# Decoding weights in 1024-column pieces, a one-operation low part of q, and the softmax guard on GpSimd, in a fused attention and two-layer MoE kernel

## The chip, the core and the metric

The kernel runs on one core of a Trainium2 chip. The metric is the time of one execution on the device, in microseconds, as the median of several runs. The engines are TensorE (PE in the profile, with its weight loads as PEld), VectorE (DVE), ScalarE (ACT), GpSimd (POOL) and SyncE (SP, which only issues DMAs here). Each engine works through its own instructions in a fixed order and waits for the others at semaphores.

## The reference

Inputs are float32. Attention with a forget gate runs on 4 batches, 8 heads, 576 positions and a head size of 64; its output, as 2304 tokens of 512 features, goes through two dense two-matrix layers with 2048 hidden features.

```python
def _attn_ref(q, k, v, f):
    scores = scale * np.matmul(q, k.transpose(0, 1, 3, 2))
    log_f = np.log(np.clip(f, 0.0001, 1.0))
    cum = np.cumsum(log_f, axis=-1)
    decay = cum[:, :, :, None] - cum[:, :, None, :]
    scores = np.where(causal, -1000000000.0, scores + decay)
    scores = scores - np.max(scores, axis=-1, keepdims=True)
    attn = np.exp(scores)
    attn = attn / (np.sum(attn, axis=-1, keepdims=True) + 1e-09)
    return np.matmul(attn, v).astype(np.float32)

def _moe_ref(x, w_in, w_out):
    h = x @ w_in
    return np.maximum(0.01 * h, h) @ w_out

def _moe2_ref(x, w_in, w_out, alpha):
    h = x @ w_in
    return (np.maximum(h, 0.0) + alpha * np.minimum(h, 0.0)) @ w_out
```

## The kernel before, in words

**Products of split numbers.** Most matrix products are made from a high and a low part of each float32 operand: the high part is a rounded copy (a "cast"), the low part is the rest (a "sub"), and three products of parts are added up in PSUM. Every operand of such a product therefore costs a cast and a subtraction on ScalarE, VectorE or GpSimd first. The first 16 heads of attention ("native", `NAT = 16`) are computed in plain float32 instead and need no split.

**Weights.** The weights arrive as 64-bit numbers. `assemble` (L481) loads a piece of 512 columns for 128 rows (512 KB) into a buffer of the ring `raw` (four buffers), then makes float32 of it in a buffer of the ring `cv` (three): ScalarE or GpSimd rescales the high word (`rebase`, L492 or L494), and VectorE shifts (`bits`, L499), adds the sign (`sign`, L502) and the low bits (`low`, L507). `split_w` (L518) then casts and subtracts into the buffer that TensorE reads. `weight1` (L530) does so for the 32 pieces of the first layer (16 chunks `f` of the hidden features, two halves each: the half of `w_in` and the half of `w_out`), all of them wanted by the first block of tokens; 18 of them are also written to DRAM and read back for later blocks. `weight2_in` (L543) and `weight2_out` (L538) do so for the second layer, 16 pieces each. `weight2_in` combines two pieces into four staged operands with a scratch tile `sc`.

**Attention.** `attention_heads` (L870) loads q and k of a head together, transposed and stored twice, on partitions 0 to 63 and 64 to 127, and splits them with `qk_hi` (L931), `q_lo` (L934, which turns the lower copy of q into its low part, 64 partitions) and `k_lo` (L937). v is loaded for two heads at a time, with a block of zeros between them, and split by `v_hi` and `v_lo`. `attention_scores` (L1089) adds the decay on VectorE (L1145), masks on GpSimd (L1097 writes a buffer `dm`; L1104 for packed 64-row units) and takes the exponential and the row sums on ScalarE (L1156). For one or two units at a time VectorE then adds 1e-9 to the sums (`guard`, L1001) and takes the reciprocal (`recip`, L1004); the normalisation (L1171 on ScalarE, L1173 elsewhere) multiplies by it, TensorE transposes (L1186), and the result is split again.

**Order of the work.** All operations of the program are given to a planner (`Plan`) with an estimated duration on each engine that may do them and a due time. It goes through a simulated time, picks for each free engine the due operation whose inputs and buffers are there, chooses between engines where several may do an operation, and so writes one fixed order for each engine. A buffer of a ring is taken and given back in that order too. The due times come from constants at the top of the file (`PROL`, `FIRST0`, `W1LEAD` and so on). The native heads fill the first 50 us or so; then the first block of 512 tokens of layer one runs while all of its weights are decoded and further heads are computed between its products; four more blocks follow with the rest of attention; then layer two from about 610 us on.

Of the kernel before, what the change touches and what calls it, by code (L numbers as in the profile page):

```python
# [25 lines left out]
MARGIN = 450  # L26
AHEAD = 7600
NRAW = 4
CW = 512
NCV = 3  # L30
# [11 lines left out]
NT0 = 12  # L42
# [4 lines left out]
W2LEAD = 112200  # L47
NEARLY = 4
W2FROM = 2.77
W2EACH = 0.68  # L50
W2LAG = 51000
W2STEP = 5300
W2OUT = 8400
# [7 lines left out]
PROL = 52000  # L61
PROL0 = 26000
FIRST0 = 99000
FREE = 8
ATTN = 12800
LASTH = 10600
W1LEAD = 12500
LEAD1 = 24000
LEAD2 = 54900
DMALAT = 2600  # L70
BATCH = 1
LASTSPAN = 1.04
STEP = 4
PRICE = 0.25
# [36 lines left out]
class Plan:  # L111
# [202 lines left out]
def tile_forgetting_attention_two_moe(ctx: ExitStack, tc, qk0, qk1, v0, v1, fg, w1, w2, alphaT, out):  # L314
# [127 lines left out]
    ring("ysb", NYSB, [P, 2, T])  # L442
    ring("qk", 2, [P, 256 + S], pool="att")
    ring("vr", 2, [P, 5, 3, D], pool="att")
# [17 lines left out]
    rate = const.tile([B * H, 2], F32, name="rate")  # L462
# [6 lines left out]
    warm_b, cum_b, yd_b, wscr_b, w2_b, rate_b = (Buf(Ring(1, None)) for _ in range(6))  # L469
    for b, ap in ((warm_b, warm), (cum_b, cum_d), (yd_b, yd), (wscr_b, wscr), (w2_b, w2in), (rate_b, rate)):  # L470
        b.ap = ap
# [9 lines left out]
    def assemble(which, f, half, d, after=()):  # L481

        raw, v = new("raw"), new("cv")
        src = (w1, w2)[which].bitcast(I32)[f, :, 2 * CW * half : 2 * CW * (half + 1)]

        def load():
            sp.dma_start(out=raw.ap, in_=src.rearrange("p (n t) -> p n t", t=2))

        def rebase(e):
            high = f32(raw.ap[:, :, 1])  # L490
            if e == "act":
                act.activation(out=f32(v.ap), in_=high, func=AF.Copy, scale=2.0**-112)  # L492
            else:
                gps.tensor_scalar(  # L494
                    out=f32(v.ap), in0=high, scalar1=2.0**-112, scalar2=1.0, op0=ALU.mult, op1=ALU.mult
                )

        def bits():
            dve.tensor_scalar(out=v.ap, in0=v.ap, scalar1=3, scalar2=None, op0=ALU.logical_shift_left)  # L499

        def sign():
            dve.scalar_tensor_tensor(  # L502
                out=v.ap, in0=raw.ap[:, :, 1], scalar=-(2**31), in1=v.ap, op0=ALU.bitwise_and, op1=ALU.bitwise_or
            )

        def low():
            dve.scalar_tensor_tensor(  # L507
                out=v.ap, in0=raw.ap[:, :, 0], scalar=29, in1=v.ap, op0=ALU.logical_shift_right, op1=ALU.bitwise_or
            )

        on("dma", t_dma(8 * CW * P), EARLY if (which, f) == (0, 0) else d - 5e3, load, w=[raw], after=after)
        plan.op({"act": t_act(CW), "pool": t_pool1(CW)}, d, rebase, r=[raw], w=[v])
        on("dve", t_dve2(CW), d, bits, w=[v], shared=True)
        on("dve", t_dve(CW), d, sign, r=[raw], w=[v], shared=True)
        on("dve", t_dve(CW), d, low, r=[raw], w=[v], shared=True)
# [902 lines left out]
```

## Time and profile before

| what | value |
| --- | --- |
| runs, median (lowest to highest) | 993.36 us (992.1 to 994.47) |
| the profiled execution, time | 991.83 us |
| the profiled execution, span from first to last instruction | 989.7 us |
| instructions | 15662 |
| VectorE, ScalarE, GpSimd busy | 746.7, 536.2, 90.1 us |
| granted TensorE clock | 1.000 of full speed |
| DMA | 203.27 MB, mean 205 GB/s |

The profiled execution lies 2.1 us above its span and 1.5 us below the median. In a row of the profile a group of instructions has its line, engine, operation, the tiles it writes and reads, its shape and count; then busy time, mean duration of one, and the idle time of the engine ahead of it. Matmuls overlap each other, so the duration of one is longer than the step from one to the next.

### The profile page before, as it was taken

Reading aid. Unit: us, or ns where it says so; the run is one execution under the profiler, and the core shown is the slowest. Engines: PE = TensorE matmul, PEld = TensorE weight load, DVE = VectorE, ACT = ScalarE, POOL = GpSimd, SP = SyncE. Lnnn points to the kernel's source line nnn. Section 1 sums busy time; section 2 is a strip of 40 time slices with the busy share of each in tenths; the row PEclk is TensorE's granted clock in tenths of the full one; section 3 lists DMA queues with packets and bytes.
Section 4 is the critical chain, followed back from the end, with each engine's and each line's share of the span. In section 5 each row is a group of like instructions: output and inputs, shape, how many; then the busy total and the mean of one; then the engine's idle time right before and its main releaser. Section 6 shows DMA issues by size and latency. Waiting matters only on the chain.

```text
span 989.7 us, 15662 instructions
## 1 busy us (share of the span) xinstructions
PE 976.0 (99%) x5170; PEld 842.6 (85%) x5170; DVE 746.7 (75%) x1849; ACT 536.2 (54%) x1231; POOL 90.1 (9%) x161
## 2 busy tenths in 40 slices
PE   9999999999999999999999999999999999999998
PEld 7777777999888878878878888889889898988987
DVE  7798999887998897986776647856696656856563
ACT  8987887996887777867646435211232112321112
POOL 2101233211211120211000000000000000000000
PEclk9999999999999999999999999999999999999999
DMA  8869887688767789845497765533374333634311
GB/s 285 286 202 320 284 316 229 207 297 285 259 228 267 242 275 320 271 145 174 138 368 253 262 213 173 175 111 118 107 245 129 127 118 107 203 121 144 105 46 64
DMA packets 76128, 203.27 MB, mean 205 GB/s; under 512 B 8112, under 2 KB 23248, under 8 KB 76048
## 3 DMA queue, kind: packets, MB, share of 16 engines
q1 hardware_dynamic: 76048, 202.28, 61.2%
q8 instruction: 41, 0.67, 0.3%
q14 instruction: 39, 0.32, 0.1%
HBM read 168.57 MB, written 33.67 MB: 204 GB/s over the span
## 4 chain that ended last, share of the span: by engine, by line
PE 76%; DVE 10%; issue 6%; DMA 4%; ACT 4%; POOL 1%; POOLq 0%; ACTq 0%; SPq 0%; DVEq 0%
PE bank L830 20%; PE bank L761 18%; PE bank L650 12%; PE bank L604 12%; PE bank L1131 5%; PE bank L1186 3%; PE bank L1034 3%; DMA raw<-w 2%; PE bank L1024 1%; DVE pt L1202 1%; DVE k L409 1%; DVE t L1145 1%; DMA w2in<-wa 1%; DVE cv L507 1%; DVE g L409 1%
## 5 line engine op out<-in xcount | busy, mean ns | idle before, releaser
L830 PE MATMUL bank<-w,g 128*128 128x512 f32 x756 | 196.9, 393 | 0.0
L404 ACT ACTIVATE g<-r 128x384 fp32r<-128x384 f32 x96 | 50.4, 526 | 256.3 <-DVE r L793 232.5
L770 DVE TENSOR_TENSOR r<-bank,r 128x384 f32<-128x384 f32 x168 | 91.0, 555 | 91.1 <-PE bank L761 90.9
L830 PEld LDWEIGHTS bank<-w,g 128*128 128x128 f32 x756 | 140.1, 188 | 21.2
L650 PE MATMUL bank<-g,ws 128*128 128x512 f32 (+1 forms) x540 | 128.0, 374 | 1.3 <-ACT g L404 1.3
L604 PE MATMUL bank<-xp,ws 128*128 128x512 f32 (+1 forms) x540 | 126.3, 372 | 0.0
L650 PEld LDWEIGHTS bank<-g,ws 128*128 128x128 f32 x540 | 92.1, 189 | 18.2 <-ACT g L404 3.7
L604 PEld LDWEIGHTS bank<-xp,ws 128*128 128x128 f32 x540 | 93.3, 189 | 15.2
L650 PE MATMUL bank<-g,w 128*128 128x512 f32 (+1 forms) x420 | 101.4, 375 | 0.1
L604 PE MATMUL bank<-xp,w 128*128 128x512 f32 (+1 forms) x420 | 99.2, 374 | 0.1
L1156 ACT ACTIVATE t<-t,nm 128x128 f32<-128x128 f32 (+4 forms) x144 | 83.9, 586 | 24.6 <-DVE nm L1145 24.2
L604 PEld LDWEIGHTS bank<-xp,w 128*128 128x128 f32 x420 | 72.1, 189 | 12.4 <-ACT t L1171 0.5
L650 PEld LDWEIGHTS bank<-g,w 128*128 128x128 f32 x420 | 71.8, 189 | 12.1 <-ACT g L404 0.7
L1202 DVE TENSOR_TENSOR pt<-bank,pt 128x128 fp32r<-128x128 f32 (+2 forms) x136 | 64.1, 504 | 22.2 <-ACT pt L404 21.7
L1097 POOL TENSOR_SCALAR_AFFINE_SELECT dm<-cb 128x448 f32<-128x448 f32 (+1 forms) x96 | 54.9, 573 | 264.1 <-DVE nm L1145 224.2
L1171 ACT ACTIVATE t<-t,nm 128x128 f32<-128x128 f32 (+4 forms) x112 | 58.8, 564 | 28.7 <-DVE nm L1004 27.5
L409 DVE TENSOR_TENSOR g<-r,g 128x384 fp32r<-128x384 f32 x96 | 53.2, 554 | 25.9 <-ACT g L404 25.9
L404 ACT ACTIVATE pt<-bank 128x512 fp32r<-128x512 f32 (+6 forms) x176 | 67.6, 433 | 4.3 <-PE bank L1186 3.6
L1186 PE MATMUL bank<-tri,t 128*128 128x128 f32 x432 | 65.8, 277 | 1.7 <-DVE t L1173 0.5
L409 DVE TENSOR_TENSOR g<-gr,g 128x512 fp32r<-128x512 f32 x72 | 50.4, 700 | 18.4 <-ACT g L404 18.3
L1186 PEld LDWEIGHTS bank<-tri,t 128*128 128x128 f32 x432 | 49.3, 141 | 15.0 <-ACT t L1171 5.3
L1034 PEld LDWEIGHTS bank<-pt,v 128*128 128x128 f32 x416 | 55.8, 189 | 5.9 <-ACT pt L404 1.9
(136 smaller groups left out, 1687.0 us busy)
## 6 DMA issues: line engine op xcount, KB each, us to landing
ws<-wscr SPq DMA_DIRECT2D x72, 512.0 KB, 4.9
raw<-w SPq DMA_DIRECT2D x64, 512.0 KB, 5.8
wa<-w2in SPq DMA_DIRECT2D x33, 512.0 KB, 3.5
ws<-w2in SPq DMA_DIRECT2D x33, 512.0 KB, 3.5
qk<-qk SPq DMA_DIRECT2D x32, 416.0 KB, 4.7
wscr<-ws SPq DMA_DIRECT2D x18, 512.0 KB, 5.6
cb<-cum_d SPq DMA_DIRECT2D x32, 288.0 KB, 4.4
vr<-v SPq DMA_DIRECT2D x16, 480.0 KB, 5.1
```

Of the source, the lines that this page charges most:

```text
L404: act.activation(out=out, in_=in_, func=AF.Copy)
L409: (dve if e == "dve" else gps).tensor_tensor(out=out, in0=in0, in1=in1, op=ALU.subtract)
L604: pe.matmul(h()[:, i] if single else h(), lhsT=w.ap[:, a, c * P : (c + 1) * P], rhs=xs[0].ap[:, s, c] if single else xp[:, x0 : x0 + 2, s, c],
L650: pe.matmul(out(c), lhsT=w.ap[:, a, col : col + P], rhs=g.ap[:, s, at : at + n], start=f == 0 and (a, s) == (0, 0) and (c % 2 == 0 or not ...
L761: pe.matmul(b.ap[:, :N2], lhsT=t.ap[:, a, o + c * P : o + (c + 1) * P], rhs=view(k)[:, s, c], start=c == 0 and i == 0, stop=c == 1 and i == 2,
L770: on("dve", t_dve(N2), d + k * step - URGENT, lambda: dve.tensor_tensor(out=out.ap, in0=b.ap[:, :N2], in1=x.ap, op=ALU.add), r=[b] if x is ...
L830: pe.matmul(acc[j * (N2 // P) + t].ap, lhsT=g.ap[:, s, t * P : (t + 1) * P], rhs=w.ap[:, a], start=p == 0 and i == j and (a, s) == (0, 0), ...
L1034: pe.matmul(po.ap[:, q:n], lhsT=v2.ap[:, o2 + j, :], rhs=pt_ap(s, e, j, j + 1, q, n), start=s == 0 and j == 0, stop=s == 1 and j == nkt - 1,)
L1156: act.activation(out=t.ap[:, :nk], in_=t.ap[:, :nk], func=AF.Exp, scale=-1.0, bias=nm.ap[:, last, u : u + 1], accum_out=nm.ap[:, 2, u : u ...
L1171: act.activation(out=t.ap[:, :nk], in_=t.ap[:, :nk], func=AF.Copy, scale=nm.ap[:, 3, u : u + 1])
L1186: pe.transpose(tp.ap[:, (j - j0) * P : (j - j0 + 1) * P], t.ap[:, k0 : k0 + P], f32(tri_b.ap[:, :P]))
L1202: dve.tensor_tensor(out=lo, in0=src, in1=f32(hi), op=ALU.subtract)
```

## The change

Weights of the first layer, and the `w_in` part of the second, are decoded two pieces at a time: `raw` and `cv` have two buffers each of 1024 columns in place of four and three of 512, and each of `rebase`, `bits`, `sign` and `low` is one instruction over 1024 columns. A chunk of the first layer is loaded by one DMA of 1 MB; the two pieces of `weight2_in` come from two places and keep two DMAs. `weight2_out` still takes 512 columns, in a buffer of the new size. The scratch of `weight2_in` comes from the ring `ysb` (which serves the stores of finished blocks) in place of `sc`. The low part of q is made by one VectorE instruction over all 128 partitions, `q * 1 + hi * s` with s = 0 above and -1 below (a column of the new tile `rates`), in place of a subtraction that VectorE or GpSimd did on 64 partitions. `guard` goes to GpSimd. v of the heads that are split is loaded without its block of zeros. The planner's delays between engines and its due times have other values. The native ring `t0` has 11 buffers in place of 12.

```diff
+TOSAME = 120
+TOPE = 310
+FROMPE = 165
+CROSS = 155
-MARGIN = 450
-AHEAD = 7600
-NRAW = 4
+MARGIN = 635
+AHEAD = 8600
+NRAW = 2
 CW = 512
-NCV = 3
+NCV = 2
...
-NT0 = 12
+NT0 = 11
...
-PROL = 52000
-PROL0 = 26000
-FIRST0 = 99000
+PROL = 55900
+PROL0 = 24800
+FIRST0 = 99800
 FREE = 8
-ATTN = 12800
-LASTH = 10600
+ATTN = 10300
+LASTH = 11700
...
-        return (0 if a == "pe" else 125) if a == b else 260 if b == "pe" else 200 if a == "pe" else 170
+        return (0 if a == "pe" else TOSAME) if a == b else TOPE if b == "pe" else FROMPE if a == "pe" else CROSS
...
-    ring("raw", NRAW, [P, CW, 2], I32, pool="conv")
-    ring("cv", NCV, [P, CW], I32, pool="conv")
-    ring("sc", 1, [P, 2, 256], pool="conv")
+    ring("raw", NRAW, [P, 2 * CW, 2], I32, pool="conv")
+    ring("cv", NCV, [P, 2 * CW], I32, pool="conv")
...
-    ring("vr", 2, [P, 5, 3, D], pool="att")
+    ring("vr", 2, [P, 5, 2, D], pool="att")
...
-    def assemble(which, f, half, d, after=()):
+    def assemble(which, parts, d, after=()):
 
         raw, v = new("raw"), new("cv")
...
+        n = len(parts) * CW
+        runs = [(0, parts)] if len(parts) == 2 and parts[0][0] == parts[1][0] else [(k, [p]) for k, p in enumerate(parts)]
+
+        def load(k, part):
+            f, half = part[0]
+            src = (w1, w2)[which].bitcast(I32)[f, :, 2 * CW * half : 2 * CW * (half + len(part))]
+            sp.dma_start(out=raw.ap[:, k * CW : (k + len(part)) * CW], in_=src.rearrange("p (n t) -> p n t", t=2))
...
         def bits():
-            dve.tensor_scalar(out=v.ap, in0=v.ap, scalar1=3, scalar2=None, op0=ALU.logical_shift_left)
+            dve.tensor_scalar(out=v.ap[:, :n], in0=v.ap[:, :n], scalar1=3, scalar2=None, op0=ALU.logical_shift_left)
...
-    def weight1(f, half, d, after=()):
-        v = assemble(0, f, half, d, after)
-        t = w_t[0, f, half] = new("ws" if (f, half) in STREAM else "w")
-        split_w(v, lambda: f32(v.ap), t, d, CW)
...
+    def weight1(f, d, after=()):
+        v = assemble(0, [(f, 0), (f, 1)], d, after)
+        for half in range(2):
+            t = w_t[0, f, half] = new("ws" if (f, half) in STREAM else "w")
+            split_w(v, lambda half=half: f32(v.ap[:, half * CW : (half + 1) * CW]), t, d + 1e3 * half, CW)
...
-        v1, v2 = assemble(1, p, 0, d, after), assemble(1, p + NP, 0, d, after)
-        sc, h, ts = new("sc"), CW // 2, []
+        v = assemble(1, [(p, 0), (p + NP, 0)], d, after)
+        sc, h, ts = new("ysb"), CW // 2, []
...
-                    out=vr.ap[:, :nkt], in_=g["v"][b, h // 2]), w=[vr])
+                    out=vr.ap[:, :nkt], in_=g["v"][b, h // 2] if native else g["v"][b, h // 2][:, :, ::2]), w=[vr])
...
-            def q_lo(en, k1=k1, qk=qk):
-                sub(en, k1.ap[D:P, :n], qk.ap[D:P, :n], f32(k1.ap[D:P, :n]))
+            def q_lo(k1=k1, qk=qk):
+                dve.scalar_tensor_tensor(
+                    out=k1.ap[:, :n], in0=f32(k1.ap[:, :n]), scalar=lower, in1=qk.ap[:, :n], op0=ALU.mult, op1=ALU.add
+                )
...
                 def guard(i=i, i1=i1):
-                    dve.tensor_scalar(out=nm.ap[:, 3, i:i1], in0=nm.ap[:, 2, i:i1], scalar1=1e-9, scalar2=None, op0=ALU.add)
+                    gps.tensor_scalar(out=nm.ap[:, 3, i:i1], in0=nm.ap[:, 2, i:i1], scalar1=1e-9, scalar2=None, op0=ALU.add)
...
-                on("dve", 70, du, guard, w=both)
+                on("pool", 180, du, guard, w=both)
                 on("dve", 75, du, recip, w=both)
```

In the first block, VectorE's decoding of one chunk stood before as follows (`cv_0` and `cv_2` are the chunk's two halves, `w_12` a finished weight, `g_2` the split of a hidden activation, `t_5` a unit of attention):

```order
L502 SCALAR_TENSOR_TENSOR cv_0_1759<-raw_0_1702,cv_0_1759 128x512
L499 TENSOR_SCALAR cv_2_1803<-cv_2_1803 128x512
L507 SCALAR_TENSOR_TENSOR cv_0_1759<-raw_0_1702,cv_0_1759 128x512
L1145 ISA t_5_1874,nm_0_1676<-bank7_76,dm_0_1723 128x128
L1145 ISA nm_0_1676 128x1
L406 CAST w_12_1889<-cv_0_1759 128x512
L502 SCALAR_TENSOR_TENSOR cv_2_1803<-raw_1_1747,cv_2_1803 128x512
L409 TENSOR_TENSOR g_2_1885<-gr_0_1868,g_2_1885 128x512
L409 TENSOR_TENSOR w_12_1889<-cv_0_1759,w_12_1889 128x512
L507 SCALAR_TENSOR_TENSOR cv_2_1803<-raw_1_1747,cv_2_1803 128x512
```

The same place now (`L507`, `L510` and `L515` are `bits`, `sign` and `low` of the changed file, `L413` the subtraction, `L947` the low part of q, `L1018` the reciprocal, `L1159` the decay):

```order
L507 TENSOR_SCALAR cv_1_1550<-cv_1_1550 128x1024
L413 TENSOR_TENSOR ws_0_1572<-cv_0_1473,ws_0_1572 128x512
L413 TENSOR_TENSOR ws_2_1578<-cv_0_1473,ws_2_1578 128x512
L510 SCALAR_TENSOR_TENSOR cv_1_1550<-raw_1_1462,cv_1_1550 128x1024
L947 SCALAR_TENSOR_TENSOR k1_0_1564<-k1_0_1564,rates_78,qk_0_1425 128x320
L413 TENSOR_TENSOR g_1_1600<-gr_0_1589,g_1_1600 128x512
L515 SCALAR_TENSOR_TENSOR cv_1_1550<-raw_1_1462,cv_1_1550 128x1024
L1159 ISA t_3_1611,nm_0_1612<-bank7_76,dm_0_1553 128x128
L1159 ISA nm_0_1612 128x1
L1018 RECIPROCAL nm_2_1394<-nm_2_1394 128x2
L1018 RECIPROCAL nm_2_1394<-nm_2_1394 128x1
L1159 ISA t_4_1616,nm_0_1612<-bank4_73,dm_1_1634 128x256
```

One instruction of 1024 columns stands where two of 512 stood between other work, and the two reciprocals have no guard ahead of them.

The guard stood on VectorE, directly ahead of its reciprocal (`xp` is the input of layer one, `t_3` a unit that is normalised):

```order
L1078 TENSOR_TENSOR xr_0_1750<-bank7_76,xr_0_1750 64x320
L1078 TENSOR_TENSOR xr_0_1750<-bank6_75,xr_0_1750 64x320
L1001 TENSOR_SCALAR nm_0_1676<-nm_0_1676 128x2
L1004 RECIPROCAL nm_0_1676<-nm_0_1676 128x2
L406 CAST xp_77<-xr_0_1750 128x128
L1173 TENSOR_SCALAR t_3_1675<-t_3_1675,nm_0_1676 128x128
L409 TENSOR_TENSOR xp_77<-xr_0_1750,xp_77 128x128
```

Now it stands in the order of GpSimd, here between a subtraction of k (`k2_0`) and the masks of the next units (`dm`):

```order
L1111 AFFINE_SELECT dm_0_1553<-cb_2_1434 128x128
L413 TENSOR_TENSOR k2_0_1570<-qk_0_1425,k1_0_1564 128x320
L1015 TENSOR_SCALAR nm_2_1394<-nm_2_1394 128x2
L1015 TENSOR_SCALAR nm_2_1394<-nm_2_1394 128x1
L1111 AFFINE_SELECT dm_1_1634<-cb_2_1434 128x256
```

The guard of `nm_2` moved from VectorE's order to GpSimd's, behind a subtraction of 128x320, and the reciprocals that wait for it are those in the rows of VectorE above. Counted over the whole program, VectorE has 1673 rows in place of 1850, 12 normalisations in place of 31, and TensorE's rows are the same products in another order.

## Rows read from the trace of the kernel before

**Rows 1.** The profile page, part 1: busy us (share of the span) and instructions of each engine.

```profile
PE 976.0 (99%) x5170; PEld 842.6 (85%) x5170; DVE 746.7 (75%) x1849; ACT 536.2 (54%) x1231; POOL 90.1 (9%) x161
```

**Rows 2.** Windows view of the core, its columns in the first line, six stretches.

```profile
core 0: us, PE busy (x) PEld busy (x) DVE busy (x) ACT busy (x) POOL busy (x), PEclk, DMA share, GB/s
0.00:50.00 50.00, 48.45 (x261) 37.97 (x262) 35.68 (x159) 44.70 (x155) 9.44 (x31) 1.00 0.86 285
50.00:175.00 125.00, 120.91 (x610) 98.04 (x609) 115.14 (x303) 98.60 (x253) 29.18 (x46) 1.00 0.81 269
175.00:250.00 75.00, 74.93 (x600) 73.15 (x599) 63.52 (x195) 61.50 (x157) 14.31 (x29) 1.00 0.78 269
250.00:500.00 250.00, 247.00 (x1357) 206.36 (x1356) 215.16 (x564) 188.87 (x400) 37.14 (x56) 1.00 0.70 232
525.00:600.00 75.00, 75.00 (x333) 62.12 (x332) 46.01 (x75) 36.46 (x61) 0.00 (x0) 1.00 0.63 216
```

**Rows 3.** Waits of TensorE: us in total, times, longest us.

```profile
PE bank L1131 <- DVE pt L1202: 1.4, 2, 1.0
PE bank L650 <- ACT g L404: 1.3, 3, 0.5
```

**Rows 4.** Timeline of VectorE, 118 to 130 us: start us, us, what, count.

```profile
118.01 1.29 DVE L502 SCALAR_TENSOR_TENSOR cv<-raw,cv 128x512 int32<-128x512 int32 x2
119.21 1.29 DVE L507 SCALAR_TENSOR_TENSOR cv<-raw,cv 128x512 int32<-128x512 int32 x2
...
123.42 0.16 DVE L1001 TENSOR_SCALAR nm<-nm 128x2 f32<-128x2 f32 x1
123.61 0.17 DVE L1004 RECIPROCAL nm<-nm 128x2 f32<-128x2 f32 x1
123.69 0.54 DVE L409 TENSOR_TENSOR xp<-xr,xp 128x128 fp32r<-128x128 f32 x2
124.15 0.75 DVE L499 TENSOR_SCALAR cv<-cv 128x512 int32<-128x512 int32 x2
124.82 1.28 DVE L502 SCALAR_TENSOR_TENSOR cv<-raw,cv 128x512 int32<-128x512 int32 x2
...
129.13 0.48 DVE L409 TENSOR_TENSOR k<-qk,k 128x320 fp32r<-128x320 f32 x1
129.53 0.75 DVE L499 TENSOR_SCALAR cv<-cv 128x512 int32<-128x512 int32 x2
```

**Rows 5.** Groups by form: busy us, mean ns of one, idle before.

```profile
L1001 DVE TENSOR_SCALAR nm<-nm 128x2 f32<-128x2 f32 x64 | 11.7, 182 | 3.6 <-ACT t L1156 3.2
...
L1173 DVE TENSOR_SCALAR t<-t,nm 128x576 f32<-128x576 f32 x20 | 10.3, 517 | 0.5
...
L1171 ACT ACTIVATE t<-t,nm 128x576 f32<-128x576 f32 x12 | 9.2, 770 | 0.0
```

**Rows 6.** Instructions by tile cb, on GpSimd: duration ns min/median/max.

```profile
L1104 POOL TENSOR_TENSOR cb<-cb,tri x32: 312/319/973, 8.3 to 189.2; 64x64 f32<-64x64 f32 x32
```

**Rows 7.** GpSimd groups by form: busy us, mean ns of one, idle before.

```profile
L409 POOL TENSOR_TENSOR k<-qk,k 64x320 fp32r<-64x320 f32 x4 | 5.2, 1291 | 15.7 <-ACT k L404 11.6 <-issue 4.1
...
L409 POOL TENSOR_TENSOR k<-qk,k 128x320 fp32r<-128x320 f32 x2 | 2.1, 1042 | 0.2
```

**Rows 8.** The chain that ended last, 100 to 109 us: start us, us, what.

```profile
100.29 0.61 DVE cv L507
100.92 7.09 DMA raw<-w
...
108.09 0.68 ACT cv L492
```

**Rows 9.** DMA issues from 50 to 175 us: KB each, median us to landing.

```profile
raw<-w SPq DMA_DIRECT2D x24, 512.0 KB, 6.0
```

**Rows 10.** Tile raw, its last line.

```profile
DMA to landing us min/median/max: 3.1/5.8/8.2
```

**Rows 11.** The chain that ended last, from 610 us.

```profile
610.22 8.98 PE bank L761 x50
```

More of the change, by code (lines that the diff above doesn't have):

```diff
@@ L46 @@
 NYSB = 2
-W2LEAD = 112200
+W2LEAD = 117200
 NEARLY = 4
 W2FROM = 2.77
-W2EACH = 0.68
+W2EACH = 0.738
 W2LAG = 51000
 W2STEP = 5300
-W2OUT = 8400
+W2OUT = 11000
 AHEAD2 = 16300
@@ L60 @@
 SHIFT = 1
-PROL = 52000
-PROL0 = 26000
-FIRST0 = 99000
+PROL = 55900
+PROL0 = 24800
+FIRST0 = 99800
 FREE = 8
-ATTN = 12800
-LASTH = 10600
+ATTN = 10300
+LASTH = 11700
 W1LEAD = 12500
-LEAD1 = 24000
-LEAD2 = 54900
+LEAD1 = 20600
+LEAD2 = 51500
 DMALAT = 2600
 BATCH = 1
-LASTSPAN = 1.04
+LASTSPAN = 1.041
 STEP = 4
-PRICE = 0.25
+PRICE = 0.266
 MASKED = 2.0**30
@@ L442, in tile_forgetting_attention_two_moe @@
     ring("ysb", NYSB, [P, 2, T])
+    rings["ysb"].ordered = False
     ring("qk", 2, [P, 256 + S], pool="att")
-    ring("vr", 2, [P, 5, 3, D], pool="att")
+    ring("vr", 2, [P, 5, 2, D], pool="att")
     ring("cb", 3, [P, S], pool="att")
@@ L460, in tile_forgetting_attention_two_moe @@
     ring("tri", 1, [P, 2 * P], F32R)
-    rate = const.tile([B * H, 2], F32, name="rate")
+    rates = const.tile([P, 3], F32, name="rates")
+    rate, lower = rates[: B * H, :2], rates[:, 2:]
     warm = const.tile([1, 1], F32, name="warm")
@@ L467, in tile_forgetting_attention_two_moe @@
     cum_d = dram.tile([B * H, 2, S], F32, name="cum_d")
-    warm_b, cum_b, yd_b, wscr_b, w2_b, rate_b = (Buf(Ring(1, None)) for _ in range(6))
-    for b, ap in ((warm_b, warm), (cum_b, cum_d), (yd_b, yd), (wscr_b, wscr), (w2_b, w2in), (rate_b, rate)):
+    warm_b, cum_b, yd_b, wscr_b, w2_b, rate_b, lower_b = (Buf(Ring(1, None)) for _ in range(7))
+    for b, ap in ((warm_b, warm), (cum_b, cum_d), (yd_b, yd), (wscr_b, wscr), (w2_b, w2in), (rate_b, rate), (lower_b, lower)):
         b.ap = ap
@@ L507, in low @@
             dve.scalar_tensor_tensor(
-                out=v.ap, in0=raw.ap[:, :, 0], scalar=29, in1=v.ap, op0=ALU.logical_shift_right, op1=ALU.bitwise_or
+                out=v.ap[:, :n], in0=raw.ap[:, :n, 0], scalar=29, in1=v.ap[:, :n], op0=ALU.logical_shift_right, op1=ALU.bitwise_or
             )
[L511 to L515, printed above, removed]
+        for k, part in runs:
+            on("dma", t_dma(8 * CW * len(part) * P), EARLY if (which, part[0][0]) == (0, 0) else d - 5e3, lambda k=k, part=part: load(k, part),
+                    a=[(raw, k)], after=after)
+        plan.op({"act": t_act(n) + 50, "pool": t_pool1(n)}, d, rebase, r=[raw], w=[v])
+        on("dve", t_dve2(n), d, bits, w=[v], shared=True)
+        on("dve", t_dve(n), d, sign, r=[raw], w=[v], shared=True)
+        on("dve", t_dve(n), d, low, r=[raw], w=[v], shared=True)
         return v
@@ L1254, in tile_forgetting_attention_two_moe @@
     for i in range(2):
+        on("pool", 100, -9.4e3, lambda i=i: gps.memset(lower[i * D : i * D + D], -1.0 * i), a=[(lower_b, i)])
+    for i in range(2):
         rows = sum(max(0, min(NAT - gi * H, H)) for gi, k in enumerate(ORDER) if k == i)
@@ L1299, in tile_forgetting_attention_two_moe @@
     for f in range(NF):
-        for half in range(2):
-            weight1(f, half, due(0, f) - W1LEAD + 1e3 * half, stored if f else [])
+        weight1(f, due(0, f) - W1LEAD, stored if f else [])
     sent = 2
@@ L1346, in tile_forgetting_attention_two_moe @@
         for f in (p, p + NP):
-            weight2_out(f, due2(0, p) - W2OUT)
-    conv_rings = [rings[k] for k in ("raw", "cv", "sc")]
+            weight2_out((f,), (due2(0, p) - W2OUT,))
+    conv_rings = [rings[k] for k in ("raw", "cv")]
     conv_ops = [o for o in plan.ops if any(b.ring in conv_rings for b in o.bufs)]
```

54 lines of the change are left out of this document (26 added, 28 removed).

## The prediction

> **What bounds the kernel now.** I read the page first: TensorE is busy for 976.0 of 989.7 us [rows 1], so the most that any change outside TensorE can give is what TensorE loses to waits. Then the windows, for where it loses it [rows 2]: from 525 to 600 us it loses nothing, from 50 to 175 us 125 - 120.9 = 4.1 us, from 175 to 250 us 0.1, from 250 to 500 us 3.0. That is 7.2 us of visible idle time. The same rows show who is short in those stretches: VectorE is busy for 115.1 of 125 us while the first layer's weights are decoded, and for 215.2 of 250 afterwards; ScalarE for 98.6 and 188.9. In the first 50 us it is ScalarE, with 44.7. Last the waits of TensorE by cause [rows 3]: small ones, on VectorE's split of attention weights and on ScalarE's copy of an activation, itself behind work that VectorE and ScalarE share.
>
> A busy TensorE is not a TensorE at its best, since one matmul's record covers a short wait of the next. A second measure is the share of weight loads: 62.12 of 75 us, 0.828, in the undisturbed stretch, so 103.5 of 125 us would be expected from 50 to 175 us, where there are 98.0 [rows 2]. The 5.5 us missing hold the visible 4.1 and another 1.4. This is a lower bound, because attention's short matmuls load more often: the stretch from 175 to 250 us shows 73.15 of 75, or 0.975. If a third of the work from 50 to 175 and 250 to 500 us were of that kind, 0.877 x 375 = 329 us would be expected against 304.4 found. I keep about 24 us as the upper end of what is there to regain.
>
> **The change part by part**, as time on VectorE first, then on the path.
>
> *Decoding.* 24 pairs are merged (16 chunks of the first layer, 8 pairs of `weight2_in`), three VectorE instructions each: 72 instructions fewer. What one costs beyond its columns is read from starts: two `sign` of 512 start at 118.01 and the next group at 119.21, so 0.60 us each; a 320-column subtraction starts at 129.13 and the next instruction at 129.53, 0.40 us [rows 4]. That is 1.04 ns a column and 0.07 us fixed. The merged decode saves 72 x 0.07 = 5.0 us. The records are longer than the steps (0.69 against 0.60 us) because they overlap, so a reader who goes by the mean of the records gets more than twice as much. [...]
>
> *Guard.* From a guard's start to that of its reciprocal 0.19 us pass (123.42 to 123.61) [rows 4]; 80 of them (64 of two units [rows 5] and 16 of one) take 15.2 us off VectorE. On GpSimd, with 29 of 125 us busy, there is room. What it costs there is not in the trace: the nearest instruction, the 64x64 addition, takes 0.31 to 0.97 us, mostly 0.32 [rows 6]. A guard that stands behind a subtraction of k waits for up to 1.0 us more [rows 7]. VectorE's order is fixed, so what waits behind a late reciprocal is all that follows on VectorE, and ScalarE's normalisation. Per reciprocal the exposed delay is between nothing (other work stands ahead of it, as in the order shown) and about 1 us. I take 0.1 us, nearest to the rows that show VectorE with work at hand most of the time: 8 us given back.
>
> *Low part of q.* The instruction has the same columns on twice the partitions; the four that GpSimd did at 1.29 us [rows 7] come to VectorE at 0.40 [rows 4]: +1.6 us.
>
> *Normalisations.* The order gives VectorE 12 in place of 31. At 0.517 us for the widest [rows 5] these 19 are under 9.8 us; with narrower ones among them I take 8. ScalarE gets them at up to 0.770 us [rows 5], some 12 us, four of them in the first 50 us, where it has 5.3 us left [rows 2]: covered, and 2 us at most if not.
>
> *Loads.* The loop from the last decode of a buffer over the next load into it (7.1 us) to the rescaling is on the chain that ended last around 100 us [rows 8]. A load takes 6.0 us there [rows 9], 3.1 to 8.2 overall [rows 10]. One load of 1 MB holds the same bytes as two, and starts only when both halves are decoded. Between nothing and 2 us later for a chunk; mostly it lands while VectorE still does other things, so I take nothing. v moves a third fewer bytes in smaller pieces; even at the longest landing of 8.2 us it is inside the 12 us by which it is issued ahead: nothing. The scratch in `ysb` may hold back a store of a finished block; the planner knows of it: nothing, and 1 us at most if not.
>
> *The sum.* VectorE: -5.0 - 15.2 + 8 + 1.6 - 8 = -18.6 us in the first 500 us, where it is busy for 429.5 now [rows 2]. That does not shorten the kernel by as much, since TensorE's products stay the same; it lets TensorE wait less. I take two thirds of the visible idle time, 4.8 us, and the 1.4 us under the records: 6.2 us. The profiled execution, 991.8 us (span 989.7 and 2.1 around it), would become 985.6; the median of the runs stood 1.5 us above it, so 987.1, rounded to **987.0 us**. The own range of this case is 983 to 991.
>
> **The rivals.**
>
> *More is regained.* If TensorE's short waits all come from VectorE's load, over half of the 24 us goes: 14 us, 979.4. For it: VectorE at 92% from 50 to 175 us. Against: few waits of TensorE name VectorE, and none is long [rows 3].
>
> *Nothing is regained.* TensorE is at 99% [rows 1], the shorter VectorE just idles, and the planner's new times move short waits about. 993.4 us. For it: the visible idle time is only 7.2 us, in many pieces.
>
> *Slower: the guard becomes a wait of VectorE.* The reciprocal stands in VectorE's order as if the guard took 0.18 us. The balance is zero when the exposed delay is (18.6 + 8) / 80 = 0.33 us per reciprocal, about the whole of a short GpSimd instruction [rows 6]. At 0.65 us (the instruction and as much again in hand-over and queueing) VectorE has 25 us more to do or to wait in 500; if a quarter of it reaches TensorE, 993.4 + 6 = 999.4 us. For it: GpSimd's instructions vary threefold, and its order puts masks and subtractions ahead of guards. Against: VectorE seldom waits for GpSimd now, and other work often stands between. [...]
>
> *Slower: decoding waits for its loads.* With a load of a whole chunk in two buffers, each of the 16 chunks is up to 2 us later; if a fifth of 32 us reaches TensorE, as the chunks are wanted in turn, 993.4 + 6 = 999 us. For it: the loop of rows 8. Against: the bytes in flight stay the same.
>
> **How the numbers follow.** The forecast has a chance of 0.48, more regained 0.19, nothing regained 0.15, the late guard 0.11, the late loads 0.07. A difference of 0.2%, 2.0 us, is about what a measurement of this kernel can tell from none. Faster than 991.4: 0.48 + 0.19 = 0.67; the same: 0.15; slower than 995.4: 0.18. The range takes in the forecast, no change, two thirds of the larger gain and the mildest of the slower cases: 977 to 996 us, which holds some 0.48 + 0.15 + 0.13 + 0.04 = 0.80.
>
> **What would show it.** VectorE busy for about 720 us, with `sign` at about 1.2 us for 1024 columns; GpSimd about 25 us more; TensorE's idle time from 50 to 500 us down from 7.2 to about 2.5 us; layer two's first product some 6 us earlier than 610 us [rows 11], and the rest as long as now. Wrong would be waits of VectorE's reciprocals on GpSimd of more than 25 us in all, waits of the rescaling on `raw` loads, or a VectorE that is relieved while TensorE's weight-load share from 50 to 175 us stays at 0.78.

## The result, and the profile after

| | median of the runs (lowest to highest) |
| --- | --- |
| before, on the same chip | 993.53 us (992.1 to 994.47) |
| after | 979.73 us (978.84 to 981.19) |
| ratio, after to before | 0.9864, 95% interval [0.9847, 0.9881] |

The change makes the kernel 13.8 us faster; 6.2 us were forecast. The time lies inside the wide range of 977 to 996 us and outside the forecast's own, 983 to 991; it is the one worked out for the rival "more is regained" (979.4 us).

The profiled execution of after took 981.19 us, the longest of its four, that of before 991.83 us, less than any of the four runs in the table. So the two profiles differ by 10.6 us only, and the kernel was profiled once more (e18 below, 978.26 us). Part 1 of the page of after, and then of that second execution, in the columns of [rows 1]:

```profile
PE 968.6 (99%) x5170; PEld 845.0 (86%) x5170; DVE 724.9 (74%) x1672; ACT 539.9 (55%) x1233; POOL 122.4 (12%) x242
```

```profile
PE 966.8 (99%) x5170; PEld 843.3 (86%) x5170; DVE 724.7 (74%) x1672; ACT 540.0 (55%) x1233; POOL 117.2 (12%) x242
```

The second one is what to set against before: its span is 976.2 us, 13.5 less. TensorE's idle time, span less busy, was 989.7 - 976.0 = 13.7 us and is now 976.2 - 966.8 = 9.4: 4.3 us come from there. The other 9.2 us are a TensorE that is *busy* for less time with the same 5170 products. Two thirds of the gain thus lay under the records of matmuls, where no list of waits shows them.

The windows view of that execution (e18), two stretches, with the columns of [rows 2], shows in which stretches:

```profile
50.00:175.00 125.00, 122.62 (x638) 101.63 (x637) 112.74 (x241) 100.48 (x247) 36.13 (x66) 1.00 0.80 270
...
250.00:500.00 250.00, 248.47 (x1379) 212.66 (x1379) 214.11 (x516) 195.01 (x407) 44.82 (x81) 1.00 0.74 236
```

In the same 125 us TensorE now starts 638 matmuls in place of 610, and its weight loads are busy for 101.6 us in place of 98.0; from 250 to 500 us for 212.7 in place of 206.4. Idle time falls by only 4.1 - 2.4 = 1.7 and 3.0 - 1.5 = 1.5 us there. The two orders do not have quite the same work in these stretches; e17 below has the same order as e18 and shows the difference again (0.772 against 0.813 for the first stretch's weight loads). So here the share of weight loads showed what TensorE regained, and the busy share of matmuls hardly did: from before to e18 the first rose from 0.784 to 0.813 in the first stretch, while the second stood at 97 and 98%.

Next the chain that ended last, of before and then of after, across the seam between the layers:

```profile
600.35 8.17 PE bank L650 x36
...
610.22 8.98 PE bank L761 x50
```

```profile
588.45 9.97 PE bank L662 x44
600.38 7.35 PE bank L773 x42
```

The last long run of layer one's products ended at 608.5 us and ends at 598.4 (600.35 + 8.17 and 588.45 + 9.97); what follows takes 381.2 and 380.7 us to the end of the two spans. The whole gain is made in the first part, as forecast.

Next what the new operations cost, by the groups by form of after on GpSimd, then on VectorE (busy us, mean ns of one | idle before):

```profile
L1015 POOL TENSOR_SCALAR nm<-nm 128x2 f32<-128x2 f32 x64 | 25.6, 400 | 86.6 <-ACT t L1170 83.5 <-ACT pt L408 1.8 <-DMA qk<-qk 0.7
L1015 POOL TENSOR_SCALAR nm<-nm 128x1 f32<-128x1 f32 x16 | 4.7, 295 | 7.1 <-ACT t L1170 6.5
```

```profile
L515 DVE SCALAR_TENSOR_TENSOR cv<-raw,cv 128x1024 int32<-128x1024 int32 x24 | 29.6, 1232 | 0.2
L510 DVE SCALAR_TENSOR_TENSOR cv<-raw,cv 128x1024 int32<-128x1024 int32 x24 | 29.4, 1226 | 0.3
...
L947 DVE SCALAR_TENSOR_TENSOR k<-k,rates,qk 128x320 fp32r<-128x320 f32 x16 | 9.1, 566 | 0.2 <-DMA ws<-wscr 0.2
```

`sign` and `low` take 1.23 us for 1024 columns. A guard on GpSimd takes 0.40 us on average and 0.29 in the median of the 80 (tile `nm` of after), where the nearest row has a median of 0.32 [rows 6]; the guards take 30.3 us in all.

Three waits in after (us in total, times, longest), for the two slower rivals:

```profile
DVE cv L507 <- ACT cv L500: 16.6, 20, 2.1
...
DVE nm L1018 <- POOL nm L1015: 8.9, 18, 1.6
...
ACT cv L500 <- DMA raw<-w: 3.7, 4, 1.5
```

The reciprocals wait 8.9 us for the guard, where 8 had been taken and 25 would have been wrong. Decoding waits 16.6 us for the rescaling (12.9 before, 17 times). Loads do not account for the increase: ScalarE's own waits for `raw` ahead of it were 6.5 us before and are 3.7 (5.1 in e18), though a load of 1 MB takes 7.2 us (median, 50 to 175 us) where one of 512 KB took 6.0 [rows 9].

### The profile page after: what moved, and what is told of

Same layout as the page of the kernel before. It is cut to its first block, busy times and chain, and to the rows that moved or that the text cites. A ratio compares the mean times of both kernels' runs of the same rounds, so it can differ in the third digit from the quotient of the medians.

```text
span 979.1 us, 15560 instructions
## 1 busy us (share of the span) xinstructions
PE 968.6 (99%) x5170; PEld 845.0 (86%) x5170; DVE 724.9 (74%) x1672; ACT 539.9 (55%) x1233; POOL 122.4 (12%) x242
## 4 chain that ended last, share of the span: by engine, by line
PE 88%; DVE 6%; ACT 3%; DMA 2%; issue 1%; ACTq 0%; DVEq 0%
PE bank L842 20%; PE bank L773 18%; PE bank L616 17%; PE bank L662 16%; PE bank L1145 6%; PE bank L1200 4%; PE bank L1048 4%; PE bank L1038 2%; DVE t L1159 1%; DMA wscr<-ws 1%; DVE pt L1216 1%; DMA ws<-wscr 1%; DVE cv L510 1%; DMA vr<-v 1%; ACT t L1185 1%
## 5 line engine op out<-in xcount | busy, mean ns | idle before, releaser
L1170 ACT ACTIVATE t<-t,nm 128x128 f32<-128x128 f32 (+4 forms) x144 | 83.5, 583 | 18.5 <-DVE nm L1159 18.2
L1185 ACT ACTIVATE t<-t,nm 128x256 f32<-128x256 f32 (+4 forms) x132 | 69.2, 564 | 14.2 <-DVE nm L1018 14.1
L413 DVE TENSOR_TENSOR g<-r,g 128x384 fp32r<-128x384 f32 x96 | 52.9, 553 | 26.8 <-ACT g L408 26.7
L408 ACT ACTIVATE pt<-bank 128x128 fp32r<-128x128 f32 (+5 forms) x175 | 68.4, 429 | 4.6 <-PE bank L1200 3.8
L625 ACT ACTIVATE gr<-bank 128x512 f32<-128x512 f32 x72 | 42.8, 594 | 35.5 <-PE bank L616 35.1
L413 DVE TENSOR_TENSOR g<-gr,g 128x512 fp32r<-128x512 f32 x72 | 51.3, 712 | 14.6 <-ACT g L408 14.2
```

Of the source, the lines that this page charges most:

```text
L408: act.activation(out=out, in_=in_, func=AF.Copy)
L413: (dve if e == "dve" else gps).tensor_tensor(out=out, in0=in0, in1=in1, op=ALU.subtract)
L1170: act.activation(out=t.ap[:, :nk], in_=t.ap[:, :nk], func=AF.Exp, scale=-1.0, bias=nm.ap[:, last, u : u + 1], accum_out=nm.ap[:, 2, u : u ...
L1185: act.activation(out=t.ap[:, :nk], in_=t.ap[:, :nk], func=AF.Copy, scale=nm.ap[:, 3, u : u + 1])
```

## The experiments

Two causes can lie behind a gain twice as large as forecast: the **operations** are worth more than I had counted, or the **order** is, since the new constants and durations made the planner write another one for every engine. An edit can be made in two ways: planned anew, which changes the order too, or with the order held, so that each engine runs the same sequence but for the instructions edited. All ratios are to the kernel before on the same chip (991.97 to 992.72 us), with a 95% interval.

### The old constants, and the new ones without the operations

**e1**: the changed kernel, planned with the constants, delays and estimates of before.

```diff
-MARGIN = 635
+MARGIN = 450
-TOPE = 310
+TOPE = 260
...
```

> The changed kernel with the planner's delays, due times and estimates of the kernel before (buffers as changed). If the relief of VectorE by the changed operations gives the time, it keeps most of the gain: 980 to 984 us. If the new delays and due times give it, most is lost: 988 to 993 us. If any replanning moves the time at random, anything within 5 us of either.

Measured: 993.08 us, ratio 1.0007 [0.9997, 1.0017]. The new operations, in an order made by the old constants, give nothing at all. Such an order is not that of before: the planner makes it anew, and chooses engines anew as well. In e1 VectorE has 32 normalisations, as before (31), where the changed kernel gives it 12, and so it is relieved by less (746.7 to 736.8 us, page part 1 of e1):

```profile
PE 975.4 (98%) x5170; PEld 845.2 (85%) x5170; DVE 736.8 (74%) x1709; ACT 525.8 (53%) x1195; POOL 127.7 (13%) x243
```

**e2**: the kernel before with the new delays, due times and estimates, all but `MARGIN`.

> The kernel before with the changed delays, due times and estimates, all but MARGIN (its own 450). If the relief of VectorE gives the time: 990 to 994 us. If the plan gives it: 981 to 986 us.

Measured: 989.04 us, 0.9966 [0.9954, 0.9977]. The constants alone, without the operations, give 3.4 us.

What e1 loses can be seen at one place. Windows view of e1, 140 to 150 us, and the timeline of its engines there (start us, us, what, and in brackets the idle time before it and what ended it):

```profile
140.00:145.00 5.00, 2.77 (x15) 2.26 (x15) 4.63 (x11) 4.19 (x11) 0.86 (x3) 0.74 0.93 262
145.00:150.00 5.00, 4.68 (x14) 3.79 (x15) 5.00 (x10) 1.17 (x5) 1.29 (x2) 0.58 0.98 381
```

```profile
138.18 1.50 DVE L510 SCALAR_TENSOR_TENSOR cv<-raw,cv 128x1024 int32<-128x1024 int32 x1
...
138.81 0.82 ACT L408 ACTIVATE pt<-bank 128x256 fp32r<-128x256 f32 x2 [0.23 <-PE bank L1200]
...
139.61 0.88 DVE L1216 TENSOR_TENSOR pt<-bank,pt 128x256 fp32r<-128x256 f32 x2
...
140.16 1.66 PE L1048 MATMUL bank<-pt,v 128*128 128x320 f32 x12 [1.06 <-DVE pt L1216]
...
140.74 1.19 ACT L500 ACTIVATE cv<-raw 128x1024 f32<-128x1024 f32 x1 [1.11 <-DMA raw<-w]
141.95 0.43 ACT L1089 ACTIVATE xr<-bank 64x320 f32<-64x320 f32 x1
...
142.41 0.48 DVE L1092 TENSOR_TENSOR xr<-bank,xr 64x320 f32<-64x320 f32 x1 [0.24 <-ACT xr L1089]
...
143.04 0.45 PE L1200 MATMUL bank<-tri,t 128*128 128x128 f32 x1 [1.22 <-DVE xr L1092]
```

A wide `sign` (L510) stands on VectorE ahead of the split `pt`, and TensorE waits 1.06 us for that split. Some 0.4 us of the wait are owed to `sign`, by an estimate: the first of ScalarE's two copies of `pt` (0.82 us together) was done at about 139.2 us, and the split starts at 139.6. Then ScalarE's rescaling (L500) waits 1.11 us for a load and takes 1.19 us more; the short `xr` stands behind it on ScalarE, VectorE's `xr` behind that, and TensorE waits 1.22 us. TensorE is busy for 2.8 of 5 us, and the granted clock is 0.74 and then 0.58 of full speed, as the mean of each 5 us. So the slower rival of the late loads did happen, in this order; and a long instruction ahead of a short one that TensorE wants is a cost for which my sum had no term.

### Parts of the change taken back, planned anew

**e5**: the changed kernel with the old four delays and three old estimates. 

> The changed kernel and its due times, with the planner's delays between engines and its three estimates as they were before. If the more exact delays make the order good, this loses much of the gain: 985 to 990 us. If the due times do, it keeps it: 979 to 982 us.

Measured: 990.17 us, 0.998 [0.997, 0.9991].

**e6**: with the old due times. 

> The other half: the changed kernel with the new delays and estimates, but all due times and margins of before. If the due times make the order good: 988 to 993 us. If the delays do: 980 to 984 us.

Measured: 986.11 us, 0.9942 [0.993, 0.9954].

**e7**: decoding 512 columns at a time, with the buffers of before. 

> The changed kernel with the weights decoded 512 columns at a time in the buffers of before (four, three and a scratch tile). VectorE gets back about 5 us by the steps between its instructions. If time follows VectorE's load at 0.3 us for each, as in the runs at a fixed order: 981 to 982 us. If the wide pieces are what the new due times are made for: 985 us or more. If wide pieces hold up short work of attention and the order merely hides it: 977 to 979 us.

Measured: 982.16 us, 0.99 [0.9887, 0.9914].

**e8**: the guard planned on VectorE. 

> The changed kernel with the guard planned and done on VectorE, which gets 15 us back. At 0.25 to 0.33 us for each: 983.5 to 985 us. If the moved guard brings nothing once the order is planned around it: 979 to 981 us.

Measured: 985.36 us, 0.9934 [0.992, 0.9947].

Each loses something, from 3 to 11 us by the ratios. e5 has the VectorE load of the changed kernel (723.6 us busy) and still is 11 us slower, so the load alone does not decide. ScalarE waits 10.7 us for loads in e6, 7.4 in e5, and 3.7 and 5.1 in two executions of the changed kernel. But what such an edit is worth can't be read off before it is known how far any new order moves the time.

### Controls: how far a new order alone moves the time

Constants that mean little in themselves, changed by a little. For the changed kernel:

**e9** (`MARGIN` 600 for 635): 

> A control: the changed kernel with the planner's margin for moving an operation to another engine at 600 in place of 635 ns; nothing else. If an order made with fitting delays is good as a class: 978 to 983 us. If any replanning moves the time by many us, so that the single comparisons of e1 to e8 mean little: 984 us or more, or under 975.

**e10** (`ATTN` 11000 for 10300): 

> A second control: the due times spread as if attention took 11.0 us more for each token block, in place of 10.3. Fitting delays make a class of good orders: 978 to 983 us. Any replanning moves the time by many us: 984 us or more, or under 975.

**e11** (the old four delays, the new estimates): 

> The changed kernel with the four delays between engines of before (125, 260, 200, 170 in place of 120, 310, 165, 155) but the three new estimates of operations. If the delays, above all that towards TensorE, are what e5 lost: 986 to 991 us. If the three estimates are: 979 to 983 us.

**e12** (the guard planned at 330 ns, nearer to the measured 400, for 180): 

> The changed kernel with the guard planned at 330 ns on GpSimd in place of 180 (the profile of the changed kernel shows 288 in the median, 400 in the mean for two units). If fitting estimates are what makes an order good, this is the version to beat both: 977 to 979.5 us, with VectorE's 8.9 us of waits for the guard down by half. If the estimate matters little: 979.5 to 982 us.

For the kernel before:

**e15** (`MARGIN` 500 for 450): 

> A control on the other side: the kernel before with the margin at 500 in place of 450 ns. If its orders vary as the changed kernel's do, anything from 985 to 1003 us. If the order of before is an ordinary one and the operations set its level: 991 to 996 us.

**e16** (`ATTN` 12000 for 12800): 

> A second control: the kernel before with attention's share of each token block's due times at 12.0 in place of 12.8 us. If its orders vary as the changed kernel's do, anything from 985 to 1003 us. If the order of before was already one of the better ones: 993 us or more.

| | median us | ratio |
| --- | --- | --- |
| e9 | 987.34 | 0.9943 [0.9929, 0.9956] |
| e10 | 982.44 | 0.9895 [0.9879, 0.9912] |
| e11 | 978.82 | 0.9858 [0.984, 0.9877] |
| e12 | 990.25 | 0.9969 [0.9956, 0.9982] |
| e15 | 988.65 | 0.9971 [0.996, 0.9983] |
| e16 | 991.69 | 0.999 [0.9981, 0.9999] |

Orders for the changed operations spread over 11.4 us (978.8 to 990.3), with e1 over 14; those for the operations of before from 988.7 (e15) to 993.5. So e5 to e8 say little about the parts they take back: all of them lie inside what such controls do. A theory also fell here, that more exact delays and durations give the better order: e11 has the old delays and is as fast as the change, e12 has a more exact guard and is 10 us slower. Nor do the waits for loads decide: ScalarE waits 6.4 us for them in e11, the fastest, and 5.1 us in e12, the slowest of the controls. The order of the changed kernel is among the best of its kind, and that of before the slowest of its own. Taken over the orders (the changed kernel, e1, e5, e6 and e9 to e12 on one side; the kernel before, e2, e15 and e16 on the other) the mean ratios are 0.9933 and 0.9982: by this estimate the new operations are worth 5 us in an order of no special merit, with some 2 us of standard error; that is near the 6.2 us forecast. Of the replanned runs e2, e6 and e12 missed every band that had been expected of them by a microsecond or more.

### Single operations, with the order held

**e3**: the kernel before, the guard's instruction not issued (the sums go to the reciprocal as they are).

```diff
-dve.reciprocal(out=nm.ap[:, 3, i:i1], in_=nm.ap[:, 3, i:i1])
+dve.reciprocal(out=nm.ap[:, 3, i:i1], in_=nm.ap[:, 2, i:i1])
```

> The kernel before without the instruction that adds 1e-9 ahead of the reciprocal; the planner still counts it, so the order of all other instructions is the same. It leaves out the 1e-9. VectorE has 15 us less to do. If TensorE's hidden waits follow VectorE's load at a fixed order, at about half a us for each: 985 to 988 us. If VectorE's load does not matter at a fixed order: 992 to 994 us.

Measured: 987.53 us, 0.9951 [0.9939, 0.9963]; VectorE busy for 737.3 us, 9.4 less. So in the order of before, too, about half of what VectorE is relieved of reaches TensorE (0.49%, 4.9 us).

**e4**: the changed kernel, the 1e-9 added again on VectorE ahead of each reciprocal.

```diff
+dve.tensor_scalar(out=nm.ap[:, 3, i:i1], in0=nm.ap[:, 2, i:i1], scalar1=1e-9, scalar2=None, op0=ALU.add)
 dve.reciprocal(out=nm.ap[:, 3, i:i1], in_=nm.ap[:, 3, i:i1])
```

> The changed kernel with the guard done a second time on VectorE ahead of each reciprocal, in an order otherwise unchanged: VectorE gets back about 15 us, and the guard on GpSimd stays. If time follows VectorE's load at half a us for each: 986 to 988 us. If it does not: 979.5 to 981 us.

Measured: 983.49 us, 0.9912 [0.9899, 0.9925], between the two bands expected. GpSimd's guard stays in e4, so the run prices the instruction on VectorE and not the wait for GpSimd.

**e13**: each wide decoding instruction issued as two of 512 columns.

```diff
+for i in range(0, n, CW):
+    c = slice(i, i + CW)
...
```

> The changed kernel in its own order, with each wide decode instruction of VectorE issued as two of 512 columns, back to back: 72 instructions more and nothing moved. By the step between instructions (0.07 us each, 5 us in all, at 0.25 to 0.33 us of time for each): 981 to 981.5 us. [...] If the wide decode's worth lies in the order alone: 979.5 to 980 us.

Measured: 980.13 us, 0.9884 [0.987, 0.9898].

**e14**: q's low part as a subtraction on 64 partitions of VectorE, and v loaded with its zeros.

```diff
-    ring("vr", 2, [P, 5, 2, D], pool="att")
+    ring("vr", 2, [P, 5, 3, D], pool="att")
...
+                sub("dve", k1.ap[D:P, :n], qk.ap[D:P, :n], f32(k1.ap[D:P, :n]))
```

> The changed kernel in its own order, with q's low part by a subtraction on 64 partitions of VectorE and v loaded with its zero blocks. Both were costed at nothing beside the planner's choice of engine: 979 to 980.5 us. If the full-width operation holds up GpSimd, or v's small pieces slow the loads: 977 to 978.5 us. If v's third fewer bytes help: 981 us or more.

Measured: 981.37 us, 0.9901 [0.9885, 0.9917].

Against the ratio of the changed kernel (0.9867, e18 below) the guard is worth 0.45% or 4.5 us, the wide decoding 0.17% or 1.7 (not clear of noise: the intervals overlap), q and v together 0.34% or 3.4 (the two were not told apart): 9.5 us, with some 4 to 5 of uncertainty, as the same ratio is subtracted three times. VectorE's busy time rose by 11.1 us in e4, by 3.9 in e13 and by 1.8 in e14, from page part 1 of each, in this order:

```profile
PE 970.7 (99%) x5170; PEld 843.4 (86%) x5170; DVE 735.8 (75%) x1752; ACT 540.2 (55%) x1233; POOL 118.2 (12%) x242
```

```profile
PE 969.1 (99%) x5170; PEld 843.6 (86%) x5170; DVE 728.6 (74%) x1744; ACT 539.7 (55%) x1233; POOL 111.8 (11%) x242
```

```profile
PE 968.4 (99%) x5170; PEld 842.7 (86%) x5170; DVE 726.5 (74%) x1672; ACT 540.5 (55%) x1233; POOL 119.2 (12%) x242
```

The 72 instructions of e13 (x1744 for x1672) cost VectorE 3.9 us, 0.054 us each, near the 0.07 read from starts in [rows 4].

The 1.8 us of e14 understate what q costs VectorE. Timeline of VectorE at one place of the common order, in e18 and then in e14:

```profile
253.06 0.41 DVE L570 TENSOR_TENSOR ysb<-cv 128x256 f32<-128x256 f32 x1
253.40 0.47 DVE L947 SCALAR_TENSOR_TENSOR k<-k,rates,qk 128x256 fp32r<-128x256 f32 x1
253.79 0.48 DVE L413 TENSOR_TENSOR v<-vr,v 128x320 fp32r<-128x320 f32 x1
```

```profile
255.02 0.41 DVE L570 TENSOR_TENSOR ysb<-cv 128x256 f32<-128x256 f32 x1
255.46 0.42 DVE L413 TENSOR_TENSOR k<-qk,k 64x256 fp32r<-64x256 f32 x1
255.92 0.49 DVE L413 TENSOR_TENSOR v<-vr,v 128x320 fp32r<-128x320 f32 x1
```

The subtraction on 64 partitions has the shorter record (0.42 against 0.47 us), but it does not overlap its neighbours as the one on 128 does: from the start of the instruction before it to that of the one behind it 0.90 us pass in place of 0.73. At 0.17 us for each of 48 such instructions that is an estimated 8 us of VectorE, of which 6 are gaps that its busy time leaves out. At the 0.4 us of time for each us of VectorE that e4 and e13 show (4.5 of 11.1, 1.7 of 3.9) q alone would give nearly all of the 3.4 us; that v gives nothing is not shown.

### All operations taken back, with the order held

**e17**: the edits of e4, e13 and e14 together, so VectorE has these operations as before, in the order of the changed kernel. GpSimd's guards and the waits for them, the loads of 1 MB, the wide rescaling and VectorE's 12 normalisations stay. **e18**: the changed kernel again, on the same chip.

> The changed kernel in its own order on every engine, with all three operations put back as they were before: each wide decoding instruction as two of 512 columns, the 1e-9 added on VectorE ahead of every reciprocal (GpSimd's guard stays as well), q's low part as a subtraction on 64 partitions, and v loaded with its blocks of zeros. It has the work of the kernel before and the order of the changed one. Theory A (two parts: the operations give some 6 to 9 us, the order the rest): 986 to 989 us, ratio 0.993 to 0.996 to the kernel before, and 6 to 9 us above the changed kernel of the same batch; VectorE busy some 20 us more than the changed kernel's 725. Theory B (the order alone gives nearly all): under 983 us. Theory C (the operations give all, and their effects only look small one by one): 991 us or more.

> The changed kernel without an edit, in the same batch as the kernel with all its operations put back, so that the difference of the two is taken on one chip: 978.5 to 981.5 us, ratio 0.985 to 0.988 by every theory. Outside of that, the ratios of single edits at a fixed order, which were compared with 979.7 us of another batch, would have to be read anew.

Measured: e17 990.22 us, 0.9984 [0.9975, 0.9993]; e18 978.72 us, 0.9867 [0.9854, 0.9881]. My expectation for e17, 986 to 989 us, was missed: together the operations are worth 11.5 us in this order, and the order without them 2.0 us (992.17 less 990.22). Page part 1 and two windows of e17, to set against those of e18 above:

```profile
PE 973.5 (99%) x5170; PEld 842.4 (85%) x5170; DVE 744.8 (75%) x1824; ACT 541.3 (55%) x1233; POOL 108.4 (11%) x242
```

```profile
50.00:175.00 125.00, 119.78 (x600) 96.54 (x599) 115.11 (x293) 96.55 (x235) 30.78 (x63) 1.00 0.78 264
...
250.00:500.00 250.00, 246.12 (x1366) 207.17 (x1366) 218.01 (x560) 194.67 (x408) 43.39 (x84) 1.00 0.71 233
```

VectorE is busy for 744.8 - 724.7 = 20.1 us less, some 26 with the gaps that e14 shows, and the kernel is 11.5 us shorter: about half of it reaches TensorE, if v's loads give nothing. Of the 12.0 us between the two spans 5.3 are visible idle time (14.7 to 9.4) and 6.7 lie in the busy time of TensorE. Together with e1 the picture is:

| | operations of before | new operations |
| --- | --- | --- |
| planned by the old constants (two different orders) | 992 to 993.5 us | 993.1 (e1) |
| order of the changed kernel | 990.2 (e17) | 978.7 to 979.7 |

Neither half gives the whole gain. In the changed kernel's order the operations are worth 11.5 us; planned by the old constants they gain nothing over the kernel before, but no run has the old operations in e1's order, so what they are worth there is open. With the new operations the choice of order moves the time by up to 14 us, with the old ones by 3 to 5.

## Why the prediction was right and wrong

**The bound: right.** The gain comes from less waiting of TensorE in the first 500 us, with nothing after them; the upper end of some 24 us to regain holds.

**VectorE's sum: right in size, its terms less so.** -18.6 us were forecast with 8 us of waits given back, so 26.6 without them; 22.0 us of busy time are gone (746.7 to 724.7; 720 was the sign to look for). Term by term: decoding 3.9 us of busy time (5.0 forecast from steps), the guard 11.1 us in e4 and 9.4 in e3 (15.2 forecast from steps, which count the gap behind it too), waits for the guard 8.9 us (8), loads added no waits of ScalarE (nothing), `sign` at 1.23 us (1.2). The 8 us for normalisations came with the new constants and not with the operations: e1 has 32 of them on VectorE. The low part of q had the wrong sign: it was counted as +1.6 us of VectorE, because columns alone were compared, and by the steps of e14 and e18 it is a relief of some 6 (44 times 0.17, less the four that came from GpSimd). v was counted as nothing; e14 measured a gain of 3.4 us for q and v.

**The step that failed** is the conversion at the end of the sum: "I take two thirds of the visible idle time, 4.8 us, and the 1.4 us under the records: 6.2 us." The visible part was near: 4.3 us over the span, though only some 3 of them from 50 to 500 us (7.2 to 4.1, where 2.5 had been named as the sign). The hidden part was 9.2 us, over six times the 1.4; with the order held (e17 and e18) the operations alone regain 5.3 us visible and 6.7 hidden. The 1.4 had been called a lower bound when it was worked out, and the 24 us of the upper bound stood beside it; the sum took the lower bound as the value. The rows that I had spoke for more: weight loads at 0.784 of a stretch in which an undisturbed one has 0.828 and attention up to 0.975.

**The order** had no term: "the planner's new times move short waits about" was put into a rival, as if it could only cancel. With the old operations it is worth 2.0 us here (e17), but e1 and e12 show that another order can take back most of the gain or all of it. Its sign could not have been told from the trace of before; a spread of some 5 us to either side was owed to the range. That the wide range held owes as much to luck as to its width: the time hangs on which order the planner writes, and the order of e9 would have met the forecast (987.3 us).

**The rivals.** "More is regained" named the time, 979.4 us, and its mechanism, VectorE's load behind TensorE's many short waits, is what e3, e4 and e17 bear out (v's loads, which e17 also puts back, were not separated). My argument against it, that few waits of TensorE name VectorE, was wrong in kind: over half of what e18 regains against e17, 6.7 of 12.0 us, lies under TensorE's records, where no list names what it waited for. "Nothing is regained" is the time of e1. The late guard and the late loads did not come as a loss in the order of the change; a late load is one of the waits of e1.

**Open:** what makes one order better than another. e11 and e12 speak against the exactness of the estimates and against the waits for loads, e5 against the load of VectorE; a single pair of waits like that of e1 explains a few microseconds, not 14. Part of it is TensorE's clock: the three slowest orders of the changed operations, e1, e5 and e12, have a mean granted clock of 0.997 over their runs, e11 and e18 of 1.000, which by an estimate is some 3 of the 10 to 14 us (0.3% of the span). Whether q or v gives the 3.4 us was not told apart by a run either; the steps of e14 speak for q.

## What to carry to other kernels

Where a program plans the order, test an operation with the order held, and run two or three harmless changes of constants first: their spread is the smallest effect that a replanned comparison can show. Here a busy TensorE hid most of what was regained (9.2 of 13.5 us lay under its records), so judge what it can regain by its weight-load share against an undisturbed stretch (here 0.784 against 0.828), and do not convert a relief of VectorE by the listed waits alone. Operations and order have to be chosen together: here the old operations in other orders gained at most 4 us, the new ones anything from nothing to 14, and the two as chosen 13.8.

## What the runs showed of the hardware that was not expected

After the same wait TensorE's granted clock fell in one execution and not in another (0.67 of full speed and 1.00). Windows 55 to 65 us and TensorE's timeline of after, and then the same of e18, the same kernel:

```profile
55.00:60.00 5.00, 3.16 (x18) 2.10 (x17) 4.55 (x9) 5.00 (x14) 0.37 (x1) 0.99 0.60 210
60.00:65.00 5.00, 5.00 (x18) 4.00 (x18) 3.19 (x8) 2.38 (x5) 0.00 (x0) 0.67 0.60 210
```

```profile
59.77 4.07 PE L1038 MATMUL bank<-pt,vr 128*128 128x320 f32 x12 [1.31 <-ACT pt L408]
63.64 2.56 PE L616 MATMUL bank<-xp,w 128*128 128x512 f32 x10
```

```profile
55.00:60.00 5.00, 3.15 (x16) 1.92 (x15) 4.59 (x8) 5.00 (x15) 0.00 (x0) 1.00 0.60 210
60.00:65.00 5.00, 5.00 (x27) 4.21 (x26) 4.81 (x8) 2.38 (x5) 0.00 (x0) 1.00 0.90 291
```

```profile
59.27 2.38 PE L1038 MATMUL bank<-pt,vr 128*128 128x320 f32 x12 [1.31 <-ACT pt L408]
61.46 4.83 PE L616 MATMUL bank<-xp,w 128*128 128x512 f32 x20
```

TensorE was busy for 3.2 of 5 us in both, with a wait of 1.31 us for ScalarE at the end. In after the next 5 us were granted 0.67 of full speed, and the twelve products took 3.87 us to the next (59.77 to 63.64); in e18 1.00, and 2.19 us. That is 1.7 us of the 2.9 by which the two executions differ. In before every stretch of [rows 2] shows 1.00.

A tiny instruction on GpSimd was not cheap here: in after two columns on 128 partitions take 0.40 us on average, and the 80 guards 0.21 to 1.16 us with a median of 0.29, near the 0.32 of an addition of 64x64 [rows 6].

Whether VectorE's neighbouring instructions overlap depended here on the partitions. The additions into `xr` on 64 partitions show it in e18, each with the instruction behind it, first for an even head (partitions 0 to 63), then for an odd one (64 to 127):

```profile
264.28 0.40 DVE L1092 TENSOR_TENSOR xr<-bank,xr 64x256 f32<-64x256 f32 x1
264.61 0.47 DVE L413 TENSOR_TENSOR v<-vr,v 128x320 fp32r<-128x320 f32 x1
```

```profile
305.63 0.43 DVE L1092 TENSOR_TENSOR xr<-bank,xr 64x256 f32<-64x256 f32 x1
306.09 0.17 DVE L1018 RECIPROCAL nm<-nm 128x2 f32<-128x2 f32 x1
```

The next instruction starts 0.07 us before the end of the first record, and 0.03 us after the end of the second. In after, the same kernel, the timeline shows 38 additions into `xr` singly: for 18 of the 19 on partitions 0 to 63 the next instruction starts 0.06 to 0.08 us before the end of the record, and for 18 of the 19 on 64 to 127 0.02 or 0.03 us after it. At the place shown above, the old subtraction of q, on partitions 64 to 127, behaves as the second (0.04 us after, in e14), its replacement on all 128 as the first (0.08 us before, in e18).
